# Another order for the first 480 steps of a hand-ordered attention and gated-MLP kernel, with small copies and subtractions put on other engines

## The chip, the cores and the metric

The kernel runs on one core of a Trainium2 chip. The metric is the time of one execution on the device in microseconds (us); lower is better. The core has five engines, each with an instruction queue of its own that is worked through in order: TensorE (PE, matmuls and transposes), VectorE (DVE), ScalarE (ACT), GpSimd (POOL) and SyncE (SP), which here only issues DMA transfers.

## The reference

Inputs are q, k, v of 8 batches, 8 heads, 576 positions and 64 channels, and the weights of a gated MLP.

```
scores = q k^T / 8 - slope_h * |i - j|, for 0 <= i - j < 128 only
attn   = softmax(scores);  x = attn v, heads side by side: [8, 576, 512]
h = gelu_tanh(x w_in)                      # w_in 512 x 1024
u, v = halves of h
v = (v - mean) / sqrt(var + 1e-6) * g_ln   # over the 512 columns
v = w_sg v + b_sg                          # w_sg 576 x 576, mixes positions
out = x + (u * v) w_out                    # w_out 512 x 512
```

Everything is float32. The large matmuls are made of three passes over rounded float32 pieces: each operand is split into a high half (a rounded copy) and a low half (the operand minus that copy), and high x high, high x low and low x high are added up.

## The kernel before

The work is cut into named steps: a letter for the kind, then a number. ORDER (lines 798 to 867) lists all 1769 steps by name. Line 877 issues them in that order, and `pin` (line 870) ties every instruction to the one before it on the same engine, so each engine's queue holds its steps exactly in the listed order. What may overlap is decided by data and buffers alone: an instruction starts when it has come to the head of its engine's queue and what it reads has been written.

**Attention** (class Pair, line 210) handles two heads at a time, 32 pairs n in all, four to a batch. Its steps, with the engine:

- SP: q loads q and k, L loads v (three DMAs). Pair 0 has q0 and Q0, the two parts of its load.
- PE: a and c are the two halves of the scores (from pair 5 on one step, `*`). t, T and z are transposes of the weights, V is the product with v.
- DVE: A, B, C, G select the band, add the bias and take minima. X and Y split the transposed weights into two masked parts. R makes the inverse sums.
- ACT: e, E, f, F, j are the exponentials. P copies a transposed block, x copies the result to SBUF, h makes its high half (line 361), k copies a tail (line 367).
- POOL: r, s, S scale the weights by the inverse sums; l makes the low half (line 364).

**Weights.** i0 to i7 load w_in and i8 to i11 w_out, as 64-bit words that a chain of steps turns into float32 halves (`split64`, line 178): d (ACT, three operations), b (DVE), + (POOL), H (ACT, the high half, line 194), - (the low half, line 196; odd numbers on DVE, even ones on POOL). wl, wH and w- do load, high half and low half for w_sg, tl, tH and t- for its last rows, bl, bH and b- for its bias, gb loads g_ln.

**MLP of a batch.** On PE: w{t}{c} and v are the product for v (t is a tile of rows, c one of four chunks of columns; v0{t} is the fourth chunk of batch 0), tt the rows left over, u the product for u, y the mixing of positions, Oa and O the product with w_out. A w step needs the high and low halves of chunk c (h, l of pair c; H, - of weight c). tt0 needs k0 to k3, a u step needs the low halves -4 to -7. Then nv, nt, vn, tn normalise v; uc copies u from PSUM; gm, gh, gl multiply and split; oa adds x; D stores.

**Buffers** set further waits. There are 8 PSUM banks; a PE step takes the one whose last user comes first in ORDER (line 413) and waits until that user is done. Two buffers each hold q/k and v loads, four hold weight loads (tag "g"), and a load waits in SP's queue, with all that is behind it, until its buffer is free.

So the order is written by hand; the `length` and `at` that the steps carry do not enter it. The code around the steps that the change touches:

Of the kernel before, what the change touches and what calls it, by code (L numbers as in the profile page):

```python
# [22 lines left out]
def attention_gmlp(  # L23
# [473 lines left out]
    def add_wide(k, at, dst, src, f, take_f):  # L497
# [17 lines left out]
        add(f"H{k}", "ACT", 0.55, at, go, [f"+{k}"])  # L515
        if k % 2:
            add(f"-{k}", "DVE", 0.62, at, go, [f"H{k}"], port=True)
        else:
            add(f"-{k}", "POOL", 1.26, at, go, [f"H{k}"])
# [275 lines left out]
    for b in range(B):  # L795
# [17 lines left out]
        nv11p k7 t9 O000 oa000 nv11c O030 z9 P9 nv11h O011 oa011 nv01c k5 uc100 v13 vn11 vg13 r8 s8 S9 nv31b nv31p S8 nv31c
        u111 uc111 O010 X9 nv31h vn13 T9 tt1 nv01h uc121 oa030 oa010 z8 u101 t8 P8 vn10 tj1 uc101 u110 T8 u131 uc110 tg1
        nt1b Y9 nt1c u130 nt1p uc130 nt1h u120 uc131 uc120 tn1 L9 D00 D02 q10 V9 *10 q12 q11 L10 L8 D01 x9 A10 ug1 y110
        gm110 X8 y111 gm111 B10 Y8 C10 y130 y131 gm131 G10 gm130 V8 f10 F10 E10 j10 e10 *11 A11 B11 e11 E11 R10 O031 y121
        y120 C11 G11 s10 f11 F11 j11 r10 t10 gm121 R11 X10 gm120 S10 T10 y100 gh11 z10 h9 x8 gh12 gm100 Y10 r11 gl11 s11
        y101 t11 gm101 oa031 gh13 P10 gh10 V10 x10 S11 gl12 gl10 gl13 X11 *12 Oa10 A12 B12 T11 O111 z11 O100 D03 q14 L11 q13
        l9 e12 h8 l8 j12 C12 E12 f12 h10 l10 P11 oa111 Y11 G12 F12 R12 oa100 Oa11 O120 V11 k10 x11 *13 r12 z12 P12 h11 k8
        s12 l11 S12 O110 A13 B13 t12 O121 O101 oa110 T12 X12 Y12 oa121 v20 v21 e13 k11 E13 vg20 vg21 k9 C13 G13 nv02b oa101  # L820
        f13 F13 j13 nv12b oa120 nv02c L12 V12 *14 D10 D11 D12 L14 q16 L13 q15 A14 R13 B14 C14 nv12p s13 r13 S13 nv02p nv12c
        G14 u200 e14 uc200 f14 u230 z13 u220 tt2 nv02h uc220 vn20 j14 nv12h vn21 E14 x12 tj2 u231 t13 X13 T13 F14 P13 v22
# [83 lines left out]
```

## Time and profile before

| | before |
|---|---|
| median of 3 runs | 594.4 us (594.01 to 594.78) |
| span of the profiled execution | 594.8 us |
| PE busy | 577.1 us, 97% of the span |
| DVE, ACT, POOL busy | 396.9, 363.5, 233.1 us |
| TensorE's mean granted clock | 0.991 of full speed |
| DMA | 47.92 MB, mean 81 GB/s |

No time of the profiled execution other than its span was kept; the span is within the runs and 0.4 us (0.07%) above their median. In the tables of the profile, an "L" number is a line of the kernel, busy time counts an engine's working time, and "idle before" is time that the engine stood still ahead of an instruction, with what ended it.

### The profile page before, as it was taken

The page shows a single profiled execution, that of the slowest core. Times are in us where ns is not written, and L with a number is a line of the kernel's source. Part 1 is how long each engine was busy: PE and PEld are TensorE (multiplying, and loading weights), DVE is VectorE, ACT ScalarE, POOL GpSimd, SP SyncE. Part 2 cuts the span into 40 slices and gives each one's busy share as a digit, 9 for nine tenths or more (in the row PEclk, how much of TensorE's full clock was granted, in tenths as well). Part 3 has the DMA queues.
Part 4 walks back from the last instruction along what each step waited for, and adds up shares of the span by engine and source line. Part 5 has one row for each costly group of instructions (what it writes and reads, how often), then busy time and mean ns, then how long its engine had stood idle before and what let it go on. Part 6 is the DMA issues. An engine that isn't in the chain of part 4 may idle for free.

```text
span 594.8 us, 16879 instructions
## 1 busy us (share of the span) xinstructions
PE 577.1 (97%) x6760; PEld 540.4 (91%) x6760; DVE 396.9 (67%) x1336; ACT 363.5 (61%) x1059; POOL 233.1 (39%) x248
## 2 busy tenths in 40 slices
PE   5789999999999999999999999999999999999997
PEld 4667999999998999999999899998999899998997
DVE  6988988566776885367757677766767577725422
ACT  7999996754664767573766348566474745632340
POOL 7877657341173223352055301634045140641130
PEclk9969999999999999999999999999999999999999
DMA  8756151030340501400324013003134004100004
GB/s 279 238 173 197 37 161 54 12 116 5 106 141 16 175 2 54 156 2 21 104 84 126 21 61 106 21 3 91 63 109 131 2 20 126 45 2 1 1 0 160
DMA packets 34898, 47.92 MB, mean 81 GB/s; under 512 B 2946, under 2 KB 24962, under 8 KB 34820
## 3 DMA queue, kind: packets, MB, share of 16 engines
q1 hardware_dynamic: 34820, 46.84, 24.4%
q8 instruction: 53, 0.87, 0.6%
q14 instruction: 25, 0.20, 0.1%
HBM read 37.39 MB, written 9.44 MB: 79 GB/s over the span
## 4 chain that ended last, share of the span: by engine, by line
PE 91%; ACT 2%; POOL 2%; DMA 2%; issue 1%; DVE 1%; SPq 1%; POOLq 0%; ACTq 0%
PE bank L571 22%; PE bank L572 22%; PE bank L573 21%; PE bank L249 7%; PE bank L334 6%; PE bank L303 4%; PE bank L339 2%; PE bank L720 1%; PE bank L719 1%; PE bank L342 1%; PE bank L655 1%; PE bank L657 1%; DMA qk<-qkT 1%; POOL g L734 1%; DMA vt<-v_in 1%
## 5 line engine op out<-in xcount | busy, mean ns | idle before, releaser
L277 ACT ACTIVATE e<-e,minima 128x128 f32<-128x128 f32 (+1 forms) x288 | 110.5, 386 | 20.9 <-DVE minima L261 20.7
L293 POOL TENSOR_TENSOR e<-e,rr 128x512 f32<-128x512 f32 (+1 forms) x96 | 75.7, 809 | 110.1 <-DVE rr L289 72.2
L261 DVE CUSTOM_DVE_ANT_0 e<-bank,bias 128x128 f32<-128x128 f32 (+1 forms) x320 | 76.0, 275 | 7.9
L571 PE MATMUL bank<-ws,vn 128*128 128x288 f32 x256 | 78.0, 305 | 0.0
L571 PE MATMUL bank<-g,wo 128*128 128x288 f32 x256 | 77.7, 304 | 0.0
L571 PE MATMUL bank<-xs,wi 128*128 128x288 f32 x256 | 77.3, 302 | 0.0
L596 POOL TENSOR_TENSOR rs<-rs,mhalf 128x1 f32<-128x1 f32 (+1 forms) x40 | 29.7, 747 | 121.3 <-DVE rs L593 118.3
L572 PE MATMUL bank<-g,wo 128*128 128x288 f32 x256 | 75.6, 295 | 0.3 <-POOL g L734 0.3
L572 PE MATMUL bank<-xs,wi 128*128 128x288 f32 x256 | 75.5, 295 | 0.0
L573 PE MATMUL bank<-ws,vn 128*128 128x288 f32 x256 | 75.5, 295 | 0.0
L573 PE MATMUL bank<-g,wo 128*128 128x288 f32 x256 | 75.4, 295 | 0.0
L572 PE MATMUL bank<-ws,vn 128*128 128x288 f32 x256 | 75.4, 294 | 0.0
L573 PE MATMUL bank<-xs,wi 128*128 128x288 f32 x256 | 75.3, 294 | 0.0
L364 POOL TENSOR_TENSOR xs<-xf,xs 128x576 fp32r<-128x576 f32 x32 | 45.9, 1441 | 67.9 <-ACT xs L361 67.9
L267 DVE COPY_PREDICATED bank<-sel,bank 128x256 f32<-128x256 uint8 x128 | 54.0, 422 | 20.0 <-PE bank L249 19.4
L249 PE MATMUL bank<-qk 64*64 64x128 f32 (+2 forms) x1536 | 55.3, 290 | 7.8 <-DMA qk<-qkT 4.7
L249 PEld LDWEIGHTS bank<-qk 64*64 64x64 f32 x1536 | 50.9, 143 | 11.4 <-DMA qk<-qkT 5.7
L734 POOL TENSOR_TENSOR g<-u,g 128x576 fp32r<-128x576 f32 x32 | 45.4, 1438 | 27.6 <-ACT g L731 27.6
L277 ACT ACTIVATION_READ_ACCUMULATOR e<-e,minima 128x1 f32 x288 | 54.3, 189 | 0.0
L311 DVE TENSOR_TENSOR px<-bank,m_own 128x512 f32<-128x512 f32 x64 | 43.7, 683 | 15.8 <-PE bank L339 9.9
L726 DVE TENSOR_TENSOR u<-bank,u 128x288 f32<-128x288 f32 x64 | 27.5, 449 | 37.4 <-PE bank L720 19.0
L571 PE MATMUL bank<-wi,xs 128*128 128x512 f32 x128 | 51.6, 403 | 0.0
(116 smaller groups left out, 1463.2 us busy)
## 6 DMA issues: line engine op xcount, KB each, us to landing
qk<-qkT SPq DMA_DIRECT2D x31, 576.0 KB, 4.7
vt<-v_in SPq DMA_DIRECT2D x32, 256.0 KB, 4.4
outT<-xf SPq DMA_DIRECT2D x28, 288.0 KB, 2.3
wst<-w_in SPq DMA_DIRECT2D x8, 512.0 KB, 5.6
vt<-v_in SPq DMA_DIRECT2D x64, 32.0 KB, 3.9
...
```

Of the source, the lines that this page charges most:

```text
L249: return lambda: nc.tensor.matmul(banks[j][half[s ^ j], dst * R:(dst + k1 - k0) * R], qk[heads[j], 0, q * R:(q + 1) * R], qk[heads[j], 1, ...
L261: nc.vector.tensor_tensor_reduce(out=dst, in0=src, in1=bs, scale=-1.0 / math.sqrt(D), scalar=3e38, op0=ALU.add, op1=ALU.min, accum_out=acc)
L267: nc.vector.copy_predicated(sv[:, :, 0:P], sels[j][:, 0:2] if t2 == 0 else sels[j][:, 1:3], sv[:, :, P:2 * P])
L277: nc.scalar.activation(x, x, AF.Exp, bias=self.nm[0:n, i:i + 1], scale=-1.0, accum_out=self.sm[0:n, i, 0:1])
L293: nc.gpsimd.tensor_tensor(x, x, self.rr[0:n, i:i + m].rearrange("p (m o) -> p m o", o=1).broadcast_to([n, m, c]), ALU.mult)
L311: nc.vector.tensor_tensor(xv[:, 0], cv, over(m_owns[j], T), ALU.mult)
L334: return lambda: nc.tensor.matmul(dst(t, s, j), vt[:, t, heads[j]], src(slice(0, P), 0, t, s, j), start=(t == 0), stop=False, skip_group_c ...
L364: nc.gpsimd.tensor_tensor(lo_of(self.xs), self.xf, hi_of(self.xs).bitcast(F32), ALU.subtract)
L571: nc.tensor.matmul(dst, ah, bh, start=(first and i == 0), stop=False)
L572: nc.tensor.matmul(dst, ah, bl, start=False, stop=False)
L573: nc.tensor.matmul(dst, al, bh, start=False, stop=(last and i == n - 1))
L734: nc.gpsimd.tensor_tensor(st[f"g{f}"][:, 1, :], st["u"][:, f, :], st[f"g{f}"][:, 0, :].bitcast(F32), ALU.subtract)
```

## The change

The first 480 entries of ORDER are put in another order. They are the same 480 names, and the other 1289 stay as they are. Seventeen steps that a new list ON_VECTOR names run on DVE. Of these, -7 and -9 were there already; k1, k2, k3, k4, h3, h4, P4, H0, H6, H7, H8, H9 and wH3 come from ACT and l3 and -4 from POOL. The odd low halves that the list does not name, -1, -3, -5 and -11, go from DVE to POOL. A high half on DVE is `tensor_copy` in place of an activation.

```diff
+    ON_VECTOR = set("""
+        k1 k2 h3 l3 k3 P4 h4 k4 H0 -4 H6 H7 -7 wH3 H8 H9 -9
+    """.split())
+
+    def copier(name):
+        return nc.vector.tensor_copy if name in ON_VECTOR else nc.scalar.copy
+
+    def lower_half(name):
+        return nc.vector if name in ON_VECTOR else nc.gpsimd
...
-        nc.scalar.activation(hi, f, AF.Copy)
+        high(hi, f)
...
-            nc.scalar.copy(hi_of(xs), self.xf)
+            copier(f"h{self.n}")(hi_of(xs), self.xf)
...
-            nc.gpsimd.tensor_tensor(lo_of(self.xs), self.xf, hi_of(self.xs).bitcast(F32), ALU.subtract)
+            lower_half(f"l{self.n}").tensor_tensor(lo_of(self.xs), self.xf, hi_of(self.xs).bitcast(F32), ALU.subtract)
...
-            got["steps"] = split64(dst[0], dst[1], got["w"], f(), nc.vector if k % 2 else nc.gpsimd)
+            got["steps"] = split64(dst[0], dst[1], got["w"], f(), copier(f"H{k}"), lower_half(f"-{k}"))
...
     ORDER = """
-        q0 i0 Q0 q1 wl3 a0 c0 A0 d0 B0 b0 C0 G0 e0 j0 E0 wH3 f0 F0 +0 w-3 a1 A1 c1 R0 B1 C1 s0 S0 r0 z0 t0 T0 i4 G1 i1 d4 b4
-        d1 j1 E1 F1 f1 H0 e1 b1 +4 X0 Y0 L0 i5 q2 +1 -0 P0 a2 c2 V0 q3 wl2 q4 i2 L1 L2 i3 gb R1 A2 B2 C2 G2 s1 r1 S1 d5 H4
-        e2 E2 j2 f2 F2 t1 z1 T1 -4 b5 a3 A3 R2 B3 X1 +5 s2 S2 r2 x0 P1 d2 j3 h0 wH2 c3 b2 t2 z2 T2 C3 Y1 a4 G3 A4 e3 H1 E3
-        d3 f3 F3 w-2 +2 l0 -1 b3 wl0 i7 q5 i6 V1 +3 R3 H2 wH0 P2 x1 H3 h1 e4 d6 s3 X2 Y2 w20 c4 t3 B4 V2 C4 r3 S3 w10 T3 z3
-        l1 X3 -2 x2 h2 P3 l2 b6 d7 E4 H5 f4 j4 w-0 w21 Y3 G4 F4 *5 w11 A5 L3 V3 L4 i11 q7 tl b7 +7 L5 i10 x3 -3 R4 B5 C5 G5
-        h3 e5 H7 E5 f5 F5 s4 l3 +6 -7 -5 w30 w22 w00 w31 w12 w32 v03 t4 w01 w02 v02 v01 H6 -6 k2 tH j5 X4 vg03 k3 vg01 d11
-        u000 S4 t- r4 R5 nv30b nv30p nv10b nv30c nv10p nv10c T4 v00 u001 nv30h k1 nv10h vn03 b11 +11 wl1 vn01 wH1 vg02 uc000
-        k0 vg00 nv20b nv20c nv00b nv20p r5 s5 nv00p Y4 nv00c u030 u031 z4 tt0 uc001 uc031 d10 nv20h uc030 P4 u020 nv00h t5
-        i8 bl vn02 b10 +10 vn00 tj0 V4 i9 q6 d8 uc020 u021 tg0 uc021 H10 u010 z5 H11 S5 T5 w-1 -10 uc010 bH P5 x4 X5 nt0b
-        nt0p Y5 nt0c u011 V5 nt0h d9 uc011 x5 -11 *6 b- tn0 b8 A6 b9 B6 +8 +9 ug0 H8 -8 H9 y000 y001 y011 y010 gm000 C6 G6
...
+        q0 i0 a0 A0 q1 B0 d0 Q0 b0 a1 c0 e0 E0 +0 tl A1 B1 j0 e1 tH C0 G0 E1 H0 i5 f0 F0 c1 R0 i1 d5 C1 i3 q2 t-
+        s0 G1 gb t0 b5 S0 j1 r0 T0 z0 X0 +5 -0 f1 F1 R1 Y0 a2 d1 H5 P0 r1 s1 A2 S1 c2 B2 L0 i4 b1 C2 t1 d3 V0 G2
+        L1 E2 d4 b3 q3 T1 z1 b4 i2 a3 -5 +1 +4 X1 x0 L2 j2 Y1 +3 h0 c3 P1 f2 wl1 F2 e2 V1 l0 A3 R2 B3 q4 i7 C3
+        d2 H1 x1 b2 G3 e3 r2 s2 S2 +2 h1 w00 z2 t2 T2 -1 P2 w10 w30 X2 j3 f3 l1 F3 E3 wH1 Y2 a4 A4 H2 V2 c4 w01
+        x2 R3 B4 k0 h2 C4 s3 w11 r3 e4 z3 G4 t3 S3 X3 l2 -2 i6 q5 T3 w31 wl3 j4 L3 P3 F4 d7 Y3 *5 b7 A5 E4 L5 f4
+        w32 w02 w12 H3 d6 R4 B5 C5 wH3 V3 x3 b6 h3 l3 k2 w-1 +7 s4 t4 e5 G5 k3 H7 i10 i11 S4 E5 r4 k1 -3 w20 T4
+        w21 X4 -7 H4 +6 f5 H6 F5 v01 w22 -4 w-3 -6 v02 j5 R5 v03 tt0 v00 wl0 L4 z4 u021 vg01 vg03 s5 d10 Y4
+        nv10b t5 S5 r5 u000 wl2 d11 wH2 P4 nv30b b10 nv10c nv30c nv10p b11 nv30p nv10h uc000 vn01 nv30h uc021
+        vg00 vn03 +10 +11 u030 vg02 wH0 uc030 nv00b H11 u020 V4 i8 nv20b z5 nv00p i9 nv00c nv20c u031 H10 T5 x4
+        u001 X5 u010 P5 nv20p u011 nv00h uc031 nv20h q6 vn00 w-0 vn02 bl tj0 Y5 q7 d8 -11 -10 uc001 tg0 w-2 V5
+        uc010 nt0b uc011 uc020 bH nt0c nt0p nt0h x5 b- d9 ug0 tn0 *6 A6 y010 y020 y001 b8 b9 B6 C6 j6 +9 H9 G6
...
```

## Rows read from the trace of the kernel before

**Rows 1.** The page, busy time of PE, its share of the span and its instructions.

```profile
PE 577.1 (97%) x6760; PEld 540.4 (91%) x6760; DVE 396.9 (67%) x1336; ACT 363.5 (61%) x1059; POOL 233.1 (39%) x248
```

**Rows 2.** Stretches of the span (from:to, length), busy us of PE, weight loads, DVE, ACT and POOL with instruction counts, the granted TensorE clock (1.00 is 2.4 GHz, 0.50 is 1.2 GHz), the DMA engines' share and GB/s.

```profile
27.80:31.20 3.40, 1.80 (x31) 1.41 (x22) 3.18 (x12) 3.32 (x10) 2.29 (x3) 1.00 0.95 298
31.30:34.60 3.30, 3.06 (x52) 2.73 (x53) 3.13 (x13) 3.30 (x12) 2.68 (x3) 0.53 0.23 50
34.70:38.00 3.30, 2.27 (x46) 1.47 (x43) 3.07 (x11) 3.27 (x12) 2.06 (x2) 0.97 0.90 291
38.10:44.90 6.80, 6.18 (x92) 5.39 (x93) 4.66 (x17) 5.55 (x17) 5.27 (x6) 0.52 0.39 136
59.20:81.10 21.90, 21.90 (x299) 20.56 (x297) 19.79 (x38) 20.00 (x42) 13.75 (x15) 1.00 0.27 92
81.10:594.80 513.70, 510.19 (x5828) 482.80 (x5826) 327.68 (x1100) 289.64 (x841) 175.36 (x176) 1.00 0.20 64
```

**Rows 3.** The waits of PE: what waited, for whom, us in total, times, longest. The first two are from 0 to 80 us, the last is all that there is after 80 us.

```profile
PE bank L249 <- DMA qk<-qkT: 4.7, 2, 3.4
PE bank L249 <- ACT p L319: 1.7, 1, 1.7
...
PE bank L572 <- POOL g L734: 0.3, 1, 0.3
```

**Rows 4.** The timeline of PE: start, length, engine, line, operation, output and inputs, count, idle time before. L249 is a, c and `*`, L334 to L342 V, L571 to L573 the three passes of w, v and u.

```profile
9.20 4.28 PE L249 MATMUL bank<-qk 64*64 64x128 f32 x72 [3.38 <-DMA qk<-qkT]
...
38.72 1.55 PE L249 MATMUL bank<-qk 64*64 64x128 f32 x22 [1.75 <-ACT p L319]
...
46.78 1.55 PE L249 MATMUL bank<-qk 64*64 64x128 f32 x48
48.27 0.50 PE L571 MATMUL bank<-wi,xs 128*128 128x512 f32 x1
...
49.16 1.15 PE L334 MATMUL bank<-px,vt 128*64 128x64 f32 x32
...
50.86 0.51 PE L571 MATMUL bank<-wi,xs 128*128 128x512 f32 x1
...
53.96 0.39 PE L571 MATMUL bank<-wi,xs 128*128 128x512 f32 x1
...
56.03 0.60 PE L303 MATMUL bank<-ident,e 128*128 128x128 f32 x4
...
59.23 0.29 PE L571 MATMUL bank<-xs,wi 128*128 128x288 f32 x1
```

**Rows 5.** The timeline of DVE in the opening: A2, B2, C2, b5 (ahead of it G2), R2, B3, X1, b2, C3, then the starts of G3, B4 and B5, which follow Y1, Y2 and Y3 at once.

```profile
21.49 0.41 DVE L267 COPY_PREDICATED bank<-sel,bank 128x256 f32<-128x256 uint8 x1
...
22.61 0.41 DVE L267 COPY_PREDICATED bank<-sel,bank 128x256 f32<-128x256 uint8 x1
...
23.87 0.43 DVE L267 COPY_PREDICATED bank<-sel,bank 128x256 f32<-128x256 uint8 x1
...
25.65 0.69 DVE L190 SCALAR_TENSOR_TENSOR tmp<-tmp,wst 128x512 int32<-128x512 int32 x1
...
27.39 0.16 DVE L288 TENSOR_REDUCE rr<-sums 128x9 f32<-128x18 f32 x1
...
27.72 0.41 DVE L267 COPY_PREDICATED bank<-sel,bank 128x256 f32<-128x256 uint8 x1
...
29.06 0.69 DVE L311 TENSOR_TENSOR px<-bank,m_own 128x512 f32<-128x512 f32 x1
...
30.40 0.69 DVE L190 SCALAR_TENSOR_TENSOR tmp<-tmp,wst 128x512 int32<-128x512 int32 x1
31.01 0.42 DVE L267 COPY_PREDICATED bank<-sel,bank 128x256 f32<-128x256 uint8 x1
...
33.23 0.42 DVE L267 COPY_PREDICATED bank<-sel,bank 128x256 f32<-128x256 uint8 x1
...
40.26 0.42 DVE L267 COPY_PREDICATED bank<-sel,bank 128x256 f32<-128x256 uint8 x1
...
47.69 0.42 DVE L267 COPY_PREDICATED bank<-sel,bank 128x256 f32<-128x256 uint8 x1
```

**Rows 6.** The chain of waits: the first of the three ACT operations of d3, and, right behind the third, eight of the exponentials (a step such as e or f has four of them, so these are two steps).

```profile
33.90 0.57 ACT wst L185
...
35.75 1.54 ACT e L277 x8
```

**Rows 7.** The timeline of DVE again: a copy, the steps -1 and -3, and a b step. POOL ran l0 from 34.55 to 35.97 and +9 from 81.69 to 83.01; it stood still from 49.12 to 50.69.

```profile
3.03 0.22 DVE L132 COPY rel<-rel 64x128 f32<-64x128 f32 x1
...
3.54 0.18 DVE L136 COPY rel<-rel 64x64 f32<-64x64 f32 x1
...
35.25 1.27 DVE L196 TENSOR_TENSOR wi<-tmp,wi 128x512 fp32r<-128x512 f32 x1
...
50.53 0.68 DVE L196 TENSOR_TENSOR wi<-tmp,wi 128x512 fp32r<-128x512 f32 x1
...
82.50 1.06 DVE L190 SCALAR_TENSOR_TENSOR tmp<-tmp,wst 128x512 int32<-128x512 int32 x1
```

**Rows 8.** The timeline of POOL: r3, s3 and S3 as one row, and -2.

```profile
38.45 2.30 POOL L293 TENSOR_TENSOR e<-e,rr 128x512 f32<-128x512 f32 x3
...
42.07 1.30 POOL L196 TENSOR_TENSOR wi<-tmp,wi 128x512 fp32r<-128x512 f32 x1
```

More of the change, by code (lines that the diff above doesn't have):

```diff
@@ L64, in attention_gmlp, with where @@
     given = []
+    ON_VECTOR = set("""
[5 more added lines that the diff above has]
+        return nc.vector if name in ON_VECTOR else nc.gpsimd
+    def where(name, other):
+        return "DVE" if name in ON_VECTOR else other
     def bank():
@@ L176, in stage, with split64 @@
         return w
-    def split64(hi, lo, w, f, last):
+    def split64(hi, lo, w, f, high, last):
         w0 = w.bitcast(U32).rearrange("p (n t) -> p n t", t=2)[:, :, 0]
@@ L318, in copy_first @@
         def copy_first(self):
-            nc.scalar.copy(self.p0[R:P], self.ct0[R:P, 0:P])
+            copier(f"P{self.n}")(self.p0[R:P], self.ct0[R:P, 0:P])
         def values(self):
@@ L353, in gather @@
             xv = xf[:, R:S].rearrange("p (t s c) -> p s t c", t=T, s=2)
+            copy = copier(f"x{self.n}")
             for s, x in enumerate(self.x1):
-                nc.scalar.copy(xv[:, s], x[:, 0:T * R].rearrange("p (t c) -> p t c", t=T))
-            nc.scalar.copy(xf[:, 0:R], self.x1[0][:, T * R:T * R + R])
+                copy(xv[:, s], x[:, 0:T * R].rearrange("p (t c) -> p t c", t=T))
+            copy(xf[:, 0:R], self.x1[0][:, T * R:T * R + R])
         def high(self):
@@ L453, in put @@
         def put(op, engine, length, after, d=0.0, **kw):
-            add(f"{op}{n}", engine, length, at + d, step(op, n), [x if isinstance(x, str) else name(*x) for x in after], **kw)
+            add(f"{op}{n}", where(f"{op}{n}", engine), length, at + d, step(op, n), [x if isinstance(x, str) else name(*x) for x in after], **kw)
         b, c = n // NPAIR, n % NPAIR
@@ L514, in add_wide @@
         add(f"+{k}", "POOL", 1.26, at, go, [f"b{k}"])
[L515 to L519, printed above, removed]
+        add(f"H{k}", where(f"H{k}", "ACT"), 0.55, at, go, [f"+{k}"])
+        add(f"-{k}", where(f"-{k}", "POOL"), 1.26, at, go, [f"H{k}"], port=True)
     def add_weights():
@@ L533, in add_weights @@
             add(f"wl{c}", "SP", 0.9, at - 8.0, load, take=[("g", [f"w-{c}"])], lag=2.0)
-            add(f"wH{c}", "ACT", 0.6, at, lambda c=c, got=got: nc.scalar.activation(ws[:, 0, c, :], got["w"], AF.Copy), [f"wl{c}"])
-            add(f"w-{c}", "POOL", 1.42, at, lambda c=c, got=got: nc.gpsimd.tensor_tensor(ws[:, 1, c, :], got["w"], ws[:, 0, c, :].bitcast(F32), ALU.subtract), [f"wH{c}"])
+            add(f"wH{c}", where(f"wH{c}", "ACT"), 0.6, at, lambda c=c, got=got: copier(f"wH{c}")(ws[:, 0, c, :], got["w"]), [f"wl{c}"])
+            add(f"w-{c}", where(f"w-{c}", "POOL"), 1.42, at, lambda c=c, got=got: lower_half(f"w-{c}").tensor_tensor(ws[:, 1, c, :], got["w"], ws[:, 0, c, :].bitcast(F32), ALU.subtract), [f"wH{c}"])
         at = WS_AT + 3.0 * T
@@ L813, in attention_gmlp @@
[L813 to L822, printed above, removed]
@@ new lines, in attention_gmlp @@
+        l7 A9 f8 O011 oa011 B9 u111 v11 k7 C9 e9 E8 v12 j8 G9 F8 E9 j9 f9 vg12 vg11 O030 u100 v13 F9 O010 Oa00
+        nv21b uc100 O000 O020 nv21c nv21p uc111 nv11b R8 oa001 R9 s9 nv21h S9 r9 nv11c vn12 vg13 t9 nv11p z9
+        nv31b nv11h nv31c vn11 k5 X9 oa000 P9 nv31p s8 nv31h S8 v10 u121 vg10 r8 k6 nv01b oa020 nv01c oa021
+        nv01p vn13 T9 tt1 nv01h uc121 oa030 oa010 z8 u101 t8 P8 vn10 tj1 uc101 u110 T8 u131 uc110 tg1 nt1b Y9
+        nt1c u130 nt1p uc130 nt1h u120 uc131 uc120 tn1 L9 D00 D02 q10 V9 *10 q12 q11 L10 L8 D01 x9 A10 ug1 y110
@@ new lines, in attention_gmlp @@
+        gm110 X8 y111 gm111 B10 Y8 C10 y130 y131 gm131 G10 gm130 V8 f10 F10 E10 j10 e10 *11 A11 B11 e11 E11 R10
+        O031 y121 y120 C11 G11 s10 f11 F11 j11 r10 t10 gm121 R11 X10 gm120 S10 T10 y100 gh11 z10 h9 x8 gh12
+        gm100 Y10 r11 gl11 s11 y101 t11 gm101 oa031 gh13 P10 gh10 V10 x10 S11 gl12 gl10 gl13 X11 *12 Oa10 A12
+        B12 T11 O111 z11 O100 D03 q14 L11 q13 l9 e12 h8 l8 j12 C12 E12 f12 h10 l10 P11 oa111 Y11 G12 F12 R12
+        oa100 Oa11 O120 V11 k10 x11 *13 r12 z12 P12 h11 k8 s12 l11 S12 O110 A13 B13 t12 O121 O101 oa110 T12 X12
@@ new lines, in attention_gmlp @@
+        s18 r19 y301 y300 gm301 gm311 gm331 T19 Y19 gm300 D20 x17 h16 q20 L19 gh30 y310 z18 P18 gm310 z19 gh31
+        P19 y330 t18 gm330 V19 gh33 x19 h17 gl31 S18 gl30 gl33 *20 T18 X18 Oa31 O310 O301 A20 Y18 V18 B20 oa310
+        C20 *21 h19 l19 l17 l16 x18 k16 k17 h18 l18 E20 k19 k18 A21 G20 B21 O311 O320 e21 F20 e20 C21 f20 tt4
+        u400 u401 Oa30 E21 j20 f21 j21 oa301 uc400 uc401 R20 s20 oa320 G21 F21 tj4 v43 t20 tg4 S20 nt4b X20
+        oa311 R21 u411 T20 u431 O300 v40 r21 nt4p s21 nt4c nt4h tn4 vg43 nv34b nv34p nv34c nv34h vn43 v41 vg41
@@ new lines, in attention_gmlp @@
+        oa331 Y22 R23 s23 S23 r23 gm421 gh42 gl42 q24 D32 q25 L23 L22 D33 *24 A24 V22 B24 t23 X23 T23 z23 Y23
+        Oa41 O401 Oa40 x22 P23 e24 C24 oa401 G24 V23 *25 h22 k20 h21 l21 f24 l22 k22 E24 x23 h23 l23 F24 k23 A25
+        B25 k21 O431 O420 O410 C25 G25 tt5 tj5 u500 tg5 j24 oa410 nt5b nt5c nt5p nt5h f25 uc500 u520 u521 j25
+        uc520 E25 v51 u531 R24 tn5 oa420 oa431 e25 s24 uc531 uc521 F25 R25 v52 O400 oa400 t24 v50 v53 r24 r25
+        S24 T24 s25 S25 vg51 u501 vg52 nv15b nv25b nv25p nv15p nv25c nv15c X24 nv25h nv15h vn51 Y24 vn52 u510
@@ new lines, in attention_gmlp @@
+        vg50 z25 P25 uc501 z24 u530 P24 uc510 vg53 nv35b nv35c D40 L24 L25 q26 q27 *27 A27 nv05b B27 t25 nv05c
+        nv05p nv35p nv35h nv05h uc530 T25 C27 G27 u511 O421 vn53 oa421 vn50 F27 uc511 O430 O411 oa411 oa430 V24
+        f27 x24 *26 A26 X25 B26 E27 e27 h24 C26 j27 R27 Y25 s27 l24 y530 y500 ug5 G26 gm500 gm530 E26 F26 e26
+        j26 f26 R26 r27 s26 S27 y531 y510 gm510 S26 r26 D41 D42 L26 V25 L27 q28 q29 D43 y501 y511 gm511 z27
+        gm501 t26 gh51 gl51 X26 gm531 y520 gm520 z26 T26 Y26 P26 k24 x25 gh53 y521 t27 T27 gh50 P27 gm521 *29
@@ L867, in attention_gmlp @@
+        O721 O701 O711 O710 O730 oa700 oa721 oa731 oa701 oa710 oa711 oa730 O720 oa720 D700 D61 D62 D721 D60 D701
+        D63 D731 D710 D711 D730 D720
     """
```

88 lines of the change are left out of this document (39 added, 49 removed).

## The prediction

> **What bounds the kernel now.** I read the page first: PE is busy for 97% of the span [rows 1]. Then its waits: after 80 us it waits once, for 0.3 us; all else lies in the opening [rows 3]. The timeline of PE puts the last of those at 38.72, where V1 and a scores step had left it idle for 1.75 us; from there it runs without a gap [rows 4]. The table by stretches shows DVE and ACT nearly always busy ahead of that point [rows 2]: the attention of pairs 0 to 3 feeds PE too slowly. It also shows the granted clock at 0.5 from about 31.3 to 34.6 and from 38.1 to 44.9, each time behind a stretch in which PE had stood still for 31 to 47% [rows 2]. The entries behind the 480th are the same, and PE is the bound there, so the change is worth what PE gains up to a common point, no more.
>
> **The common point** is the first u step, 59.23 before [rows 4]. In the new order PE has T4, z4, v00 and tt0 ahead of it too. Prices: a w or v step 0.69 (three of them from 53.96 to 56.03), a transpose of four blocks 0.44, so z 0.14 and tt0, eight matmuls of 512 columns at a third of a w step, 1.84 [rows 4]. The 0.44 is an estimate: it lasts 0.60 at 56.03, but the next step overlaps part of that. Together 3.1. PE before, gapless, has done this work at 62.35. **When is it done after?**
>
> **DVE to Y3.** PE's V steps wait for Y, the last masked part, and DVE hardly idles, so I follow DVE. Prices from starts [rows 5]: A 1.12, B 1.26, C or G 0.89, R 0.33, X or Y (two operations) 1.34, b 0.61. ACT prices: d 1.85, an exponential 0.77 [rows 6].
> - The start is later. q1 now loads ahead of Q0 and a1 runs ahead of c0. Before, c0 began at 9.20, when Q0 was there, and a1 and c1 followed with no wait, 1.43 each [rows 4, 3]. So q1 was there by 10.6 and, moved forward, by about 9.4. A1 starts at 10.9; A1, B1, C0, G0 end at 15.1, one exponential later R0 can run: 16.0. R0, C1, G1, b5, X0, R1, Y0 (6.1, some waiting) bring A2 to 21.8, against 21.49. H0, now on DVE, fits into the wait ahead of R0.
> - A2 to Y1 took 11.74. The new order defers A3, R2, B3 and C3 (3.60) and does one b more: Y1 ends at 30.5, before 33.23.
> - A3, R2, B3, C3, b2, G3, X2, Y2 are 7.8: Y2 ends at 38.3, before 40.26. Gone from here are A4, R3 and -1, whose 1.27 [rows 7] is on POOL now.
> - A4, R3, B4, C4, G4, X3, Y3 are 7.2: Y3 ends at 45.5, before 47.69. There DVE had waited for PE at half clock.
>
> ACT keeps up: F1 ends at 19.8, then d1, d3, d4 (5.55), four exponential steps (3.08) and six small ones (an estimate of 2.8, a few tenths each) put what R2 waits for at 31.2; R2's turn is at 31.6.
>
> **PE beside it.** From Y2 on: V2 1.70, c4 0.75 (half of the 1.49 of `*5`), w01, w11, z3, t3, T3, w31 [rows 4], then `*5`, which takes X3's bank, to 45.7; three w's; V3 (its bank waits for A5, 47.2) to 49.4; t4, w20, T4, w21 to 51.7. Then **v01 waits for l3**, the new stop.
>
> **DVE from Y3 to the u step.** b7, A5, R4, B5, C5: 49.7. Next come wH3, b6, h3, l3, a mix the old order did not have. On the trace, a subtraction on DVE took 0.68 with POOL still and 1.27 with POOL at work, a b step 1.06 then [rows 7]. No copy of 512 columns from SBUF to SBUF is shown; from 64 and 128 columns (0.18 and 0.22) it would be 0.47, and the nearest delay, 0.59, makes 1.06. POOL works through s4, S4, r4, -3, +6 and w-3 here (2.30, then 1.3 or more each [rows 8]) until 53.9. I take l3 at 1.27, as the row, and half the delay for the copies and b6: 0.8 + 0.85 + 0.8 + 1.27, l3 ends at 53.4. So PE stands 1.7 us.
> From there: five w or v steps, tt0 and z4, 5.4, bring PE to 58.8. DVE has k2, G5, k3, H7, k1, X4 (0.2 for a k), -7 alone, H6, and -4 beside -6, 1.27: 59.0. u021 needs -4. So 59.0: **3.35 earlier** than 62.35, at full clock.
>
> **The clock.** Two waits of the new order are near the 1.75 behind which the clock was 0.5 [rows 4, 2]: 1.7 ahead of v01, and 1.5 ahead of V2, where POOL's 2.30 behind R2's 31.9 [rows 8], then T2, w10, w30 and a4 let PE stop at 36.8. In both stretches that held such idle time before, the clock itself was still near 1.00 and fell only behind them [rows 2], so which of the two waits it follows is open. I take one fall, of the shorter kind (3.3 us, half of it lost, 1.65). Behind v01 it puts PE at 60.4, gain 1.95; behind V2 it delays c4, C4 and X3 by 1.6, gain 1.75. **Forecast: 594.4 - 1.9 = 592.5 us.** The profiled execution is 0.4 above the median; the difference is taken from both.
>
> **What costs nothing here.** H8, H9, h4, k4 and P4 leave ACT for DVE, and -11 DVE for POOL, where PE never waits [rows 2]. Their cover is the PE work to the first use. The thinnest is tn0: DVE needs about 20 us from -4 to tn0 (its 19.79 of busy time from 59.2 to 81.1, which held nearly the same steps [rows 2]), and PE 20.4 from u021 to where y010 reads it (the 21.90 of [rows 2] less the 3.1 moved forward, plus 1.6 of y010). So above 3.4 the gain ends there. **DMA queue:** q2 now waits for the later c0 but is put ahead of i4 and L0; i2 waits for +5, wl3 for +2, L4 stands behind wl0, which waits for +6. By the sums each arrives four or more us ahead of its use. Before, q/k cost PE 4.7 us in two waits [rows 3]; a late q2 would show at a2.
>
> **A rule against it.** Rows 7 show the delay of 0.59 when DVE and POOL both work. The Trainium skill, "SBUF — State Buffer", section "SBUF: two separate sides", says that the two share a port pair under an exclusive lock, and that whichever comes second is held for the other's whole instruction, a DVE copy in its two-port mode included. The trace agrees on subtractions; no row shows it for a copy of this size. By it each copy would pay the full delay, and POOL too: the first rival's 594.8 and not 592.5.
>
> **Rivals.**
> - *The two engines hold each other up* (gain lost). Copies and b6 pay 0.59 each (l3 0.8 later), POOL, set back by five such, works into DVE's next steps, so k2, k3, H7, k1 and -7 pay as well, 3.0: -4 at 62.8, 594.8, or 594.0 with half of it. For it: POOL is close to full in this walk. Against: copies are short. Chance 0.22.
> - *The clock falls at V2 for as long as at 38.1, 6.8 us* (slower). V2 and c4 at half speed end at 43.2, not 40.8; C4, due at 41.0, waits; w01, w11 at half speed put t3 at 46.4, X3 3.7 late. All behind moves by 3.7, and with a short fall at v01 PE is at 64.1: 1.7 late, 596.1. It decides when the clock in c4 is 0.5 past 41. For: the wait is 1.5 against 1.75. Against: ahead of its wait PE is nearly full from 30.5 to 36.8, as it was not before. Chance 0.18.
> - *No fall* (faster still). 591.0; with the copies free of POOL l3 ends at 52 and the gain is held by tn0 at 3.4 to 4. For: dense work stands behind both waits. Against: [rows 2], as above. Chance 0.20.
>
> **How the numbers follow.** The forecast has 0.40. A measurement of this kernel tells about 0.2% (1.2 us) from no change. Faster: forecast and no fall, less their edge, 0.58. Same: most of the first rival and that edge, 0.24. Slower: 0.18. The range, 590.4 to 596.0, leaves out a gain over 4 and the worst of the slower cases; the forecast's own is 591.5 to 593.3.
>
> **What would show it.** Right: last long PE idle ahead of v01, not at a scores step; Y1 near 30.5, Y3 near 45.5; first u step near 60.4; nothing new behind. Wrong: R0 later than 17, a wait at a2 for q/k, copies on DVE above 0.8, 0.5 of clock for 6.8 us behind V2, or PE waits past 62.

## The result: 9 us slower, all of it behind the first u step

The changed kernel took 603.4 us (median of 4 executions, 602.2 to 604.5); the kernel before, beside it, 594.2. The ratio is 1.0147, with an interval of 1.0127 to 1.0166. Forecast were 592.5, with a range to 596.0.

The page of the changed kernel shows DVE with 12.7 us more than before, PE with 1.4 more [rows 1]:

```profile
PE 578.5 (96%) x6760; PEld 539.6 (90%) x6760; DVE 409.6 (68%) x1347; ACT 358.1 (59%) x1046; POOL 237.0 (39%) x250
```

Next its stretches, with the columns of [rows 2]. In the opening there is one low-clock stretch, 31.3 to 34.6, and no second one at 38. What is new stands in the last two rows: PE idles for 3.1 us of 21.9 where it had been full, while DVE is busy for 21.33 of the 21.9, and PE idles for 2.4 us more behind 81.1. Between the two stretches of the opening and these, from 45 to 59.2, the granted clock is 1.00.

```profile
31.30:34.60 3.30, 3.30 (x45) 2.73 (x42) 3.04 (x19) 3.26 (x10) 2.80 (x4) 0.57 0.82 282
38.10:44.90 6.80, 6.80 (x142) 5.81 (x140) 6.33 (x30) 5.56 (x20) 5.64 (x6) 1.00 0.43 129
45.00:59.20 14.20, 11.99 (x117) 8.46 (x110) 13.67 (x39) 10.14 (x36) 9.79 (x9) 1.00 0.45 138
59.20:81.10 21.90, 18.77 (x180) 16.68 (x180) 21.33 (x37) 16.29 (x33) 16.30 (x14) 1.00 0.39 119
81.10:100.00 18.90, 16.54 (x244) 16.09 (x245) 17.30 (x59) 13.13 (x36) 9.12 (x9) 0.97 0.28 82
```

PE's longest waits from 62 us on (columns as in [rows 3]; L329 is z, L347 to L355 V, L582 to L584 w, v, u and y, L306 r and s). Before there was 0.3 us in all behind 80:

```profile
PE bank L329 <- POOL e L306: 2.4, 1, 2.4
PE bank L347 <- DVE px L324: 2.1, 2, 1.7
PE bank L582 <- ACT vg L656: 0.6, 1, 0.6
```

The same in PE's timeline: a scores step waits 2.11 us for a masked part of pair 1 (29.20), v01 waits for h3 and l3 (53.41, 55.19), the first u step begins at 60.40, V5 stops at 81.02 for a masked part, `*6` begins at 82.61, z6 stops at 97.47:

```profile
29.20 0.88 PE L262 MATMUL bank<-qk 64*64 64x128 f32 x22 [2.11 <-DVE px L325]
...
53.41 0.50 PE L582 MATMUL bank<-wi,xs 128*128 128x512 f32 x1 [0.48 <-DVE xs L375]
55.19 0.51 PE L584 MATMUL bank<-wi,xs 128*128 128x512 f32 x1 [1.03 <-DVE xs L378]
60.40 0.38 PE L582 MATMUL bank<-xs,wi 128*128 128x288 f32 x1
...
81.02 1.15 PE L347 MATMUL bank<-px,vt 128*64 128x64 f32 x30 [1.69 <-DVE px L324]
...
82.61 1.51 PE L262 MATMUL bank<-qk 64*64 64x192 f32 x48
...
97.47 0.33 PE L329 MATMUL bank<-ident,e 128*128 128x128 f32 x1 [2.36 <-POOL e L306]
```

And DVE: b6 at 51.22, l3 at 53.39, k2 (64 columns) at 55.05, -4 at 60.06, the first statistics of the normalisation (nv10b) at 62.27, then two products of nv10c and nv30c in 2.46 us, two low halves of vn01 and vn03 in 2.45, those of vn00 and vn02 in 3.43, Y5 at 80.29, tn0 to 85.28:

```profile
51.22 1.77 DVE L203 SCALAR_TENSOR_TENSOR tmp<-tmp,wst 128x512 int32<-128x512 int32 x1
...
53.39 1.74 DVE L378 TENSOR_TENSOR xs<-xf,xs 128x576 fp32r<-128x576 f32 x1
55.05 1.41 DVE L381 CAST xs<-xs 128x64 fp32r<-128x64 f32 x1
...
57.26 0.19 DVE L381 CAST xs<-xs 128x64 fp32r<-128x64 f32 x1
...
60.06 0.69 DVE L209 TENSOR_TENSOR wi<-tmp,wi 128x512 fp32r<-128x512 f32 x1
...
62.27 0.68 DVE L602 BATCH_NORM_STATS2 st<-vg 128x6 f32<-128x512 f32 x1
...
65.36 2.46 DVE L610 SCALAR_TENSOR_TENSOR vg<-vg,mv,gb 128x512 f32<-128x512 f32 x2
...
68.34 2.45 DVE L618 SCALAR_TENSOR_TENSOR vn<-vg,rs,vn 128x512 fp32r<-128x512 f32 x2
...
75.49 3.43 DVE L618 SCALAR_TENSOR_TENSOR vn<-vg,rs,vn 128x512 fp32r<-128x512 f32 x2
...
80.29 0.67 DVE L324 TENSOR_TENSOR px<-bank,m_own 128x512 f32<-128x512 f32 x1
...
84.53 0.75 DVE L618 SCALAR_TENSOR_TENSOR vA<-vg,rs,vA 64x512 fp32r<-64x512 f32 x1 [0.36 <-ACT vA L615]
```

What POOL had in hand beside these (L546 is w-, L209 the low halves -11 and -10, L205 the + steps), and r6 with s6 and S6 at 97.12, for which z6 waits:

```profile
54.47 1.95 POOL L546 TENSOR_TENSOR ws<-wst,ws 128x576 fp32r<-128x576 f32 x1
...
65.82 1.45 POOL L205 TENSOR_TENSOR tmp<-tmp,wst 128x512 int32<-128x512 int32 x1
68.55 1.69 POOL L205 TENSOR_TENSOR tmp<-tmp,wst 128x512 int32<-128x512 int32 x1 [1.28 <-issue]
...
75.38 2.99 POOL L209 TENSOR_TENSOR wo<-tmp,wo 128x512 fp32r<-128x512 f32 x2
...
97.12 2.29 POOL L306 TENSOR_TENSOR e<-e,rr 128x64 f32<-128x64 f32 x3 [1.39 <-DVE rr L302]
```

So PE came to the first u step at the forecast time, and the loss began where the prediction had stopped looking.

### The profile page after: what moved, and what is told of

It reads as the page before. It is cut to its first block, busy times and chain, and to the rows that moved or that the text cites. A ratio compares the mean times of both kernels' runs of the same rounds, so it can differ in the third digit from the quotient of the medians.

```text
span 602.7 us, 16868 instructions
## 1 busy us (share of the span) xinstructions
PE 578.5 (96%) x6760; PEld 539.6 (90%) x6760; DVE 409.6 (68%) x1347; ACT 358.1 (59%) x1046; POOL 237.0 (39%) x250
## 4 chain that ended last, share of the span: by engine, by line
PE 80%; DVE 3%; ACT 1%; POOL 1%; issue 1%; POOLq 0%; DVEq 0%; ACTq 0%
PE bank L582 20%; PE bank L583 19%; PE bank L584 19%; PE bank L262 5%; PE bank L347 5%; PE bank L316 4%; PE bank L352 2%; PE bank L731 1%; PE bank L730 1%; PE bank L666 1%; PE bank L355 1%; PE bank L668 1%; POOL g L745 1%; PE bank L329 1%; DVE e L274 0%
## 5 line engine op out<-in xcount | busy, mean ns | idle before, releaser
L306 POOL TENSOR_TENSOR e<-e,rr 128x512 f32<-128x512 f32 (+1 forms) x96 | 75.9, 812 | 107.7 <-DVE rr L302 67.6
L582 PE MATMUL bank<-xs,wi 128*128 128x288 f32 x256 | 77.6, 303 | 0.8 <-ACT vg L656 0.6
L582 PE MATMUL bank<-ws,vn 128*128 128x288 f32 x256 | 78.1, 305 | 0.0
L582 PE MATMUL bank<-g,wo 128*128 128x288 f32 x256 | 77.5, 303 | 0.0
L584 PE MATMUL bank<-ws,vn 128*128 128x288 f32 x256 | 75.8, 296 | 0.0
L584 PE MATMUL bank<-xs,wi 128*128 128x288 f32 x256 | 75.5, 295 | 0.1
L584 PE MATMUL bank<-g,wo 128*128 128x288 f32 x256 | 75.5, 295 | 0.0
L378 POOL TENSOR_TENSOR xs<-xf,xs 128x576 fp32r<-128x576 f32 x31 | 44.0, 1427 | 64.4 <-ACT xs L375 64.0
L262 PE MATMUL bank<-qk 64*64 64x128 f32 (+2 forms) x1536 | 54.0, 284 | 6.3 <-DMA qk<-qkT 3.9
L582 PE MATMUL bank<-wi,xs 128*128 128x512 f32 x128 | 51.7, 404 | 0.8 <-DVE xs L375 0.5
```

Of the source, the lines that this page charges most:

```text
L262: return lambda: nc.tensor.matmul(banks[j][half[s ^ j], dst * R:(dst + k1 - k0) * R], qk[heads[j], 0, q * R:(q + 1) * R], qk[heads[j], 1, ...
L306: nc.gpsimd.tensor_tensor(x, x, self.rr[0:n, i:i + m].rearrange("p (m o) -> p m o", o=1).broadcast_to([n, m, c]), ALU.mult)
L378: lower_half(f"l{self.n}").tensor_tensor(lo_of(self.xs), self.xf, hi_of(self.xs).bitcast(F32), ALU.subtract)
L582: nc.tensor.matmul(dst, ah, bh, start=(first and i == 0), stop=False)
L584: nc.tensor.matmul(dst, al, bh, start=False, stop=(last and i == n - 1))
```

## The experiments

Each was timed beside the kernel before on the same chip; "+6" is a median of 6 us above that kernel's. The changed kernel stands at +9.2. The theories first: **Order** (the new sequence places steps where they must wait), **Load** (the steps given to DVE and POOL make these late), **Contention** (DVE and POOL hold each other up).

**The new order with the engines of before.**

```diff
     ON_VECTOR = set("""
-        k1 k2 h3 l3 k3 P4 h4 k4 H0 -4 H6 H7 -7 wH3 H8 H9 -9
+        -1 -3 -5 -7 -9 -11
     """.split())
```

> The new order with the engines of before: ON_VECTOR holds only -1 -3 -5 -7 -9 -11, so all copies are on ACT, l3 and -4 on POOL. Contention (POOL's subtractions stand beside the normalisation of batch 0 in the new order, and hold up DVE's operations with two SBUF inputs there): POOL still runs -10, w-0 and w-2 there, so most of the loss stays, 598 to 601 us; the two operations of vn00 and vn02, 3.43 us after, take over 2.5. Load (the fifteen operations put on DVE are what makes it late): at most 594, and the lead of some 2 us at the first u step is kept or larger. Order (the new order is bad behind the u steps whatever the engines): 601 or more, with PE's waits at V5 and z6 as after.

607.1 us, +11.8 (ratio 1.0182 to 1.0215). PE's waits up to 60 us, and the row of POOL that ends the longest: l3 waits for h3 on ACT, and s4, without which PE has no t4, stands behind l3 (with w-1 and +7 between them).

```profile
PE bank L316 <- POOL e L306: 12.9, 3, 7.7
```

```profile
52.65 1.40 POOL L378 TENSOR_TENSOR xs<-xf,xs 128x576 fp32r<-128x576 f32 x1 [6.66 <-ACT xs L375]
```

The new order needs the new engines; z6's wait, 2.9 us, is there all the same. Order's number came, but through a stop in the opening that no theory had named. V5's wait falls to 0.5 us, against Order; the two operations of vn00 and vn02 take 3.70 us, as Contention had it. So this run does not decide between the three.

**The old order with the new engines.** ORDER is that of before, ON_VECTOR that of the change.

> The order of before with the new engines. Contention: w-0 to w-3 are done early in that order, so the normalisation is mostly free of them; only copies beside POOL cost, 594 to 597. Load: DVE carries the same operations as after, 599 to 603. Order: within 1 us of before, 593 to 595.

597.2, +1.9 (1.0025 to 1.0062), just above Contention's range, and PE has no wait behind 60 us but the 0.3 that was there before. In the old order the new engines cost 1.9 and stop PE nowhere behind the opening, so the larger part of the 9.2 needs the new order.

**Less POOL work beside the normalisation.** w-0, w-2, -10 and -11 become copies on ACT; the + steps stay on POOL.

```diff
-        return nc.vector if name in ON_VECTOR else nc.gpsimd
+        return nc.scalar if name in ("-10", "-11") else nc.vector if name in ON_VECTOR else nc.gpsimd
...
+                nc.scalar.copy(ws[:, 1, c, :], got["w"]) if c in (0, 2) else ...
```

> The changed kernel with w-0, w-2, -10 and -11 as copies on ACT in place of subtractions on POOL: these four low halves hold the whole operand, not the remainder. Contention: vg and vn steps of the normalisation go back to 0.70 to 0.75 each (after: 1.2 and 1.5), tn0 ends some 4 us earlier, 598 to 600 us. Load or order: DVE has as much to do and the order is the same, 602 to 604, less at most 1.

601.8, +6.5 (1.0084 to 1.0142): above Contention's range, and within what Load or order allowed. Its waits of PE behind 62 us: V5's is gone, z6's is not, and PE now stops for tn0 (L730 is the y product that reads vA):

```profile
PE bank L329 <- POOL e L306: 2.6, 1, 2.6
PE bank L582 <- ACT vg L656: 0.6, 1, 0.6
PE bank L730 <- DVE vA L618: 0.3, 1, 0.3
```

The vn operations go from 5.9 us to 3.9 and not to 3.0, the vg operations stay at 3.9 (here beside +10 and +11), and tn0 ends at 83.65, 1.6 us earlier and not 4:

```profile
L618 DVE SCALAR_TENSOR_TENSOR vn<-vg,rs,vn 128x512 fp32r<-128x512 f32 x4 | 3.9, 1002 | 0.0
L610 DVE SCALAR_TENSOR_TENSOR vg<-vg,mv,gb 128x512 f32<-128x512 f32 x4 | 3.9, 1007 | 0.0
```

The four low halves on POOL are worth some 2.7 us by the medians (9.2 less 6.5), but the two intervals overlap (1.0084 to 1.0142 and 1.0127 to 1.0166), so the size is uncertain; what the + steps cost was not tried.

**The last copies on ACT again.** h4, k4, H8 and H9 leave the list.

```diff
-        k1 k2 h3 l3 k3 P4 h4 k4 H0 -4 H6 H7 -7 wH3 H8 H9 -9
+        k1 k2 h3 l3 k3 P4 H0 -4 H6 H7 -7 wH3 -9
```

> The changed kernel with h4, k4, H8 and H9 back on ACT. It asks about the second loss, PE's wait for z6 at 95 us: DVE has 3.1 us less between y010 and R6 (h4 1.40, H9 0.93, H8 0.42, and waits). Contention or load: R6 comes 2 to 3 us earlier, the wait of 2.36 goes and with it the half clock behind it, 599 to 601 us. Order (z6 was moved ahead of y000, y031 and y030 on PE): the wait stays over 1.5 us, 602 to 603.5.

602.6, +7.3 (1.0107 to 1.0147), Order's number; z6 still waits 2.6 us and V5 1.7. The late copies are not what z6 waits for.

**z6 later.**

```diff
-    *7 ... z6 ... s6 S6 y000 t6 gm000 X6 T6 y031 ...
+    *7 ... y000 y031 z6 ... s6 S6 t6 gm000 X6 T6 ...
```

> The changed kernel with one difference: y000 and y031, 1.6 us of PE work each, stand ahead of z6 and not behind it, so PE has 3.3 us more to do before it asks for r6. Order (the place of z6 costs what its wait and the low clock behind it show, the rest of the loss is elsewhere): the 2.4 us wait of z6 for POOL goes to under 0.5, no stretch at half clock near 100 us, 599.5 to 601.5. Load (DVE and POOL are simply late in this part, so that the next step waits instead): the wait moves to V6 or to the O steps, and the time stays at 602.5 to 604.5.

602.0, +6.9 (1.0108 to 1.0138). z6's wait is gone, and the clock is 1.00 in 81 to 100 and in 100 to 120. But V6 waits 1.5 us for its masked parts where it had waited for nothing (V7's 0.4 is gone), so that the V steps lose 3.2 us in all and not 2.1:

```profile
PE bank L347 <- DVE px L324: 3.2, 3, 1.7
```

The time is half a microsecond above Order's range, and Load's shifted wait is there too.

**New head, old tail.** The new order up to u021, then the rest in the old sequence (wl2 first, wH0 w-0 behind vg00, wH2 w-2 behind uc031, i8 bl behind +10).

> The new order up to u021, where PE was 2.3 us ahead of the kernel before, and behind it the remaining steps in the sequence of the kernel before (the two loads wl0 and wl2 with their halves, which the new head leaves over, stand between the vg and uc steps, i8 and bl behind +10). The engines are those of the changed kernel. Order (the sequence behind u021 is what loses): the lead is kept, 592 to 593.5. Load (the lead can't be kept by any sequence, since DVE is not ahead by as much): waits of PE between 62 and 100 us of 2 us or more, 594 to 596.5. Contention (w-0, w-2 on POOL beside the normalisation, which the kernel before had done earlier): normalisation operations on DVE of over 1 us each, 596 to 600.

600.1, +5.0 (1.0072 to 1.0106). Behind 81 us PE waits for little any more (0.5 us for ACT at 86.0, and the 0.3 of before); ahead of it T5 waits 2.0 us for POOL. Load's sign came, without its number; Contention's range ends at 600, but its sign did not come: vn operations took 0.76 us in the mean and vg operations 0.91.

**The same, and old engines in the tail.**

```diff
-        k1 k2 h3 l3 k3 P4 h4 k4 H0 -4 H6 H7 -7 wH3 H8 H9 -9
+        k1 k2 h3 l3 k3 H0 -4 H6 H7 -7 wH3 -9 -11
```

> The order of the run before this one; the copies P4, h4, k4, H8, H9 stay on ACT and -11 on DVE, as in the kernel before, so only the opening's steps change engines. Order: within 1 us of the run before this one, as these steps have cover. Load on DVE (the copies behind 59 us take DVE time that PE's next steps wait for): 1 to 2 us faster than it. Contention: -11 goes back beside POOL's steps, within 1 us.

598.4, +3.3 (1.0046 to 1.0076): 1.7 faster than the one before, as Load said. t5 and T5 wait 2.0 us for POOL.

**Old head, new tail.** The complement: old up to u000 with the old engines (vg01 and vg03 exchanged), then the new sequence with the new engines (wl1 first, wH1 w-1 behind vn03; k1, which stands behind u000 here, on ACT).

> The complement: the old order up to u000 with the engines of the kernel before, and behind it the remaining steps in the new sequence with the new engines (vg01 and vg03 exchanged, wl1 moved to the front, wH1 and w-1 behind vn03). PE has no lead here. Order: the wait of z6 for r6 comes back with 2 us or more, and the time is 598 to 602. Load (the loss came from the lead meeting a DVE that had none): 593.5 to 596.

603.2, +8.1 (1.0122 to 1.0161), z6 waits 2.4 us: Order's sign came, and Load's number is refuted. But the 8.1 are not all the new tail's: H10 and H11 stood ahead of x4 on ACT and cost PE 2.9 us in a wait of a size that the changed kernel does not have there. Without it some 5 us are left.

**w-0 and w-2 behind nv00p and S5** (new head, old tail, old engines).

```diff
-    vg00 wH0 w-0 nv20b nv20c nv00b nv20p r5 s5 nv00p ... uc031 wH2 w-2 ... S5 ...
+    vg00 wH0 nv20b nv20c nv00b nv20p r5 s5 nv00p w-0 ... uc031 wH2 ... S5 w-2 ...
```

> The kernel with the new head, the old tail and the old engines behind u021 lost its lead between 60 and 81 us, mostly where t5 and T5 waited for s5 and S5 on POOL, which stood behind w-0 and w-2. Here w-0 stands behind nv00p and w-2 behind S5, nothing else is changed against it. POOL's queue (these two low halves, which the old head had done before, hold up the weights): the waits of t5 and T5, 0.4 and 1.6 us, go, and the time is 595.5 to 596.8. DVE (the normalisation, which starts no earlier than in the kernel before, is the bound of this part anyway): PE waits at V5 or at the first y steps in their place, and the time stays at 597.8 to 599.

598.4, +4.0 (1.0046 to 1.0082): nothing gained. T5 still waits 1.1 us for POOL, and V4 now waits 1.0 for P4, which is late on ACT. POOL's queue alone was the wrong theory, and the time is DVE's; the waits change places.

**New order up to `*6`, then the old one.** Engines as changed.

> The changed kernel up to *6, the last step ahead of the first y steps, and behind it the remaining steps in the sequence of the kernel before; engines as changed. Two places (the changed kernel loses some 5 us between u021 and *6 and, apart from that, 4.5 to 5 behind it): no wait of z6 for POOL, PE 3.0 us behind the kernel before at *6 and as much at the end, 597 to 599.5. One cause (DVE, late from the normalisation on, would stop PE in any sequence behind *6): the shift still grows by 3 us or more behind *6, 601 to 604.

600.5, +6.1 (1.0071 to 1.0122), 1 us above Two places' range and half a microsecond below One cause's. z6's wait falls to 0.2; V5's stays:

```profile
PE bank L347 <- DVE px L324: 1.7, 1, 1.7
```

So by the medians about 3 of the 9.2 come from the sequence behind `*6`. Here `*6` begins at 82.27, 4.0 us behind the second profile of the kernel before (78.23, shown further down), and the span, 598.4 against 593.4, is 5.0 longer: 4.0 are lost by `*6` and 1.0 behind it.

**The same with less POOL work beside the normalisation** (the copies on ACT of the third experiment).

> The run before this one, and w-0, w-2, -10 and -11 are made on ACT by one copy each, so that POOL does not run beside the normalisation on DVE; these four low halves then hold the whole operand, not the remainder. Contention and place add up: what the four took from V5 when they alone were taken out of the changed kernel, some 2.5 us at *6, is gained here too, 594.5 to 596.5, and the normalisation's eight operations with two SBUF inputs take 0.75 us each. Not additive: 597 or more.

599.4, +5.0 (1.0052 to 1.0101). V5's wait goes, yet only 1.1 us are won, and each four of the stretched operations still take 3.9 us, not 3.0. The effects do not add up: with one wait gone, PE meets the next (0.6 for a vg, 0.4 for z, 0.4 for t, 0.3 for vA).

**The kernel before, profiled again.** No edit.

> The kernel before, unchanged, profiled a second time. In every run so far the time was 1.7 us above the span; the profiled execution of the kernel before had a span of 594.8 us, which is 1.9 above the median span of its other runs, 592.9. Sample (that execution had a low-clock stretch, 38.1 to 44.9, that most have not, so the sum was made against a late opening): span 592 to 593.5, no stretch of 6 us at half clock between 35 and 50 us, and the first u step at 56.8 to 58 us instead of 59.2, so that the new order's opening has no lead of 2 us to lose. Not the sample: span 594 or more, the fall at 38 us and the first u step at 59.2 again.

595.2 us, span 593.4. The clock fell at other places, in 31.3 to 38 instead of 31.3 to 34.6 and 38.1 to 44.9 [rows 2]:

```profile
31.30:34.60 3.30, 3.30 (x50) 2.84 (x50) 3.17 (x13) 3.30 (x12) 2.64 (x3) 0.50 0.17 26
34.70:38.00 3.30, 3.30 (x51) 2.37 (x47) 3.06 (x11) 3.27 (x12) 2.06 (x2) 0.64 0.90 276
38.10:44.90 6.80, 6.14 (x127) 5.13 (x127) 6.58 (x20) 6.53 (x19) 5.34 (x7) 1.00 0.58 194
```

The first u step began at 57.85 and `*6` at 78.23, each 1.38 us earlier than in the first profile [rows 4] (there `*6` stands at 79.61):

```profile
57.85 0.29 PE L571 MATMUL bank<-xs,wi 128*128 128x288 f32 x1
...
78.23 1.51 PE L249 MATMUL bank<-qk 64*64 64x192 f32 x48
```

DVE entered the normalisation at 58.88 and left it (tn0) at 79.44:

```profile
58.88 0.69 DVE L591 BATCH_NORM_STATS2 st<-vg 128x6 f32<-128x512 f32 x1 [1.49 <-ACT vg L645]
...
78.70 0.74 DVE L607 SCALAR_TENSOR_TENSOR vA<-vg,rs,vA 64x512 fp32r<-64x512 f32 x1
```

Sample held: the forecast was made against a late execution. This one is a single execution too; its span is 0.5 above the median of the kernel's other runs beside it, 592.9, that of the first profile 1.9.

**Five copies on ACT again** (to the kernel with w-0 and w-2 later).

```diff
-        k1 k2 h3 l3 k3 H0 -4 H6 H7 -7 wH3 -9 -11
+        h3 l3 H0 -4 -7 wH3 -9 -11
```

> The kernel with the new head, the old tail and w-0, w-2 later, with one difference: k1, k2, k3, H6 and H7 are made on ACT again, which stood idle for 3.7 us there, and not on DVE, where they took 2.6 us ahead of the normalisation. Load on DVE (the copies that came to DVE make the normalisation late, and with it the weights and the y steps): the first statistics operation at 58.3 to 59.5 us, not 60.8, and 596 to 597.3. Place or PE (DVE's lateness is hidden): the time stays within 0.6 of 598.4.

599.3, +4.7 (1.0057 to 1.0096): no gain, where Load had forecast one. On ACT k3 stands ahead of the last exponentials of pairs 4 and 5 and waits for l3; these, a table load of 1.28 us and the vg steps behind it come later, and with them the first statistics on DVE (60.76 before the edit):

```profile
55.12 0.24 ACT L381 CAST xs<-xs 128x64 fp32r<-128x64 f32 x1 [3.52 <-DVE xs L378]
...
59.76 1.28 ACT L656 ACT_TABLE_LOAD   x1
```

```profile
61.68 0.70 DVE L602 BATCH_NORM_STATS2 st<-vg 128x6 f32<-128x512 f32 x1 [1.49 <-ACT vg L656]
```

So taking these five copies off DVE does not bring the normalisation forward. Here k3, waiting for a late l3, held up what was queued behind it on ACT, as l3 and k2 had done on DVE.

## Why the prediction was wrong

**Right: the opening up to Y3, and the new stop.** Y3 was forecast to end at 45.5, and did at 45.68; the new stop is v01 behind l3, 1.5 us where 1.7 stood. The first u step began at 60.40, as written, and equal work (the 3.1 us are the prediction's estimate) was at 62.35 before, so PE was 1.95 us ahead there, as forecast.

**Right by luck: the 60.4.** It was made of 58.8 and 1.65 for a low clock behind v01. No such fall came: the granted clock was 1.00 from 45 to 59.2 and on to 81. The one low stretch, 31.3 to 34.6, lay ahead of both waits that the prediction had named, behind the 2.11 us of a scores step at 29.20, and DVE came to Y3 on time all the same. What made PE late was DVE: beside POOL's work b7 took 1.27 us, b6 1.77 and l3 1.74, where the walk had 0.61, 0.85 and 1.27, so l3 ended at 55.13 and not at 53.4, and -4 at 60.75 and not at 59.0. A clock term of 1.65 that did not come and a delay of 1.7 that was not reckoned cancel.

**Wrong by 1.4: what the sum was made against.** The step is "the profiled execution is 0.4 above the median; the difference is taken from both". In every run of this study the time was 1.66 to 1.80 us above the span, so the profiled execution, with its span of 594.8, took some 596.5, 2.1 above the median. The table of before sets that span against a median of times as if the two were alike. The second low-clock stretch of that execution, 38.1 to 44.9, stands at 1.00 in the second profile. Against the second profile equal work is at 57.85 + 3.1 = 60.95, and the lead is 0.55 us. With the opening as it came there was hardly anything to gain.

**Wrong by 5: the cover up to `*6`.** The step is "the thinnest is tn0: DVE needs about 20 us from -4 to tn0". -4 ended at 60.75 (forecast 59.0), and from there to the end of tn0 DVE took 24.5 us, with one wait, of 0.4. Put against the second profile of before: DVE enters the normalisation at 62.27 and not at 58.88, 3.4 late, and leaves it at 85.28 and not at 79.44, 5.8 late. The 3.4 were in view: PE's lead was reckoned at the u step, but the normalisation hangs on DVE, and the change gives DVE eight copies and two low halves (l3, -4) ahead of it, puts Y4 ahead of it, and takes three low halves away. Inside the normalisation 2.4 more are lost. The stretching adds 3.9 there, while Y4 and -11, which stood inside before, now stand elsewhere. Four operations of each kind, with busy time and mean ns, in the changed kernel and then in the second profile of before:

```profile
L618 DVE SCALAR_TENSOR_TENSOR vn<-vg,rs,vn 128x512 fp32r<-128x512 f32 x4 | 5.9, 1508 | 0.0
L610 DVE SCALAR_TENSOR_TENSOR vg<-vg,mv,gb 128x512 f32<-128x512 f32 x4 | 3.9, 1006 | 0.0
```

```profile
L607 DVE SCALAR_TENSOR_TENSOR vn<-vg,rs,vn 128x512 fp32r<-128x512 f32 x4 | 3.0, 746 | 0.2 <-ACT vn L604 0.2
L599 DVE SCALAR_TENSOR_TENSOR vg<-vg,mv,gb 128x512 f32<-128x512 f32 x4 | 2.9, 757 | 0.0
```

That is 3.9 us more, beside -11, -10, +10, +11 and two w- steps on POOL. Y5 stands behind all of it in DVE's queue, V5 waits, and at `*6` PE is 4.4 us behind the second profile (82.61 against 78.23), having come 0.55 ahead: 4.9 lost. V5's wait is 1.7 of these. Smaller waits for ACT and POOL (0.6, 0.3, 0.3 and 0.2) make 1.4, and the other 1.8 are longer busy time for the same work (19.08 us against 17.28). Without V5's wait PE would not have got far: tn0 ended at 85.28 and PE read vA at 85.74, and in the third experiment, with V5's wait gone, it stopped for tn0 instead. So DVE's end of the normalisation bounds this part, as the prediction's own condition said, with 24.5 us where it had put 20. The prediction counted these moves at nothing since PE "never waits" there, a reading of the old order; and DVE's 19.79 of 21.90 in that stretch [rows 2] had said that no room was left for them.

**Wrong by 4.9: the sequence behind `*6`.** It was not walked at all. Before, y020 and y030 stand between `*7` and z6; now z6 follows `*7` at once, while its weights need R6 on DVE (96.57, behind -9 and a gm step) and then r6 on POOL (97.12). The 2.4 us wait is followed by a granted clock of 0.72 in 98 to 104, 1.7 us of loss in 6:

```profile
98.00:104.00 6.00, 6.00 (x37) 5.98 (x36) 5.78 (x25) 4.32 (x18) 4.21 (x4) 0.72 0.04 15
```

The fall does not always follow: in the profile of the third experiment z6 waited 2.6 us, and the clock stayed at 1.00 from 81 to 120. The spans of the two profiles differ by 9.3 (602.7 and 593.4): -0.55, +4.9 and, as what is left, +4.9. (The two executions took 0.9 and 0.6 us more than the medians beside them, so the profiles' 9.3 may stand for the 9.2 of the medians.) The old sequence behind `*6` took away 3.1 of it by the medians and 3.9 by the profiles.

**The rivals.** The first, two engines that hold each other up, had the right mechanism and the wrong place: k2 took 1.41 us beside w-1 where k3 took 0.19 alone, but h3, k3, H7 and k1 were not touched, l3 and the b steps were; the larger price fell due behind the u step. Here the Trainium skill, "SBUF — State Buffer", section "SBUF: two separate sides", states that the two share a port pair under an exclusive lock, and that, where both need it, whichever starts second is blocked for the other's whole instruction. The trace agrees for k2: it ends at 56.46, w-1 at 56.42. The second, slower by a clock fall at V2, did not happen: the granted clock behind V2, from 38.1 to 44.9, was 1.00. The third, no fall, had nothing to show, as one came at 31.3. Of the signs listed as wrong two came: a copy on DVE above 0.8 (k2), and PE waits past 62.

**What stays open.** A new head with the old tail and tail engines still loses 3 to 4 us, with waits that move between POOL, ACT and DVE when one cause is taken away. That it is the lateness of l3 and of the normalisation fits these runs, but it is not shown: no run moved l3 earlier alone, and none took the + steps from beside the normalisation. No version beat the kernel before.
